# Attention sums guarded on VectorE across partitions, all probability copies on ScalarE

## The chip, the cores and the metric

The kernel runs on one core of one Trainium2 chip. The metric is the device time of that core in microseconds (us), the median of the runs shown. One execution was profiled; its trace is what is read here.

## The reference

There are 8 batches, 8 heads, a sequence of 576 and a head size of 64. Causal attention with a decay is followed by a layer in which 128 of the 576 tokens of each batch go through a two-layer network.

```python
scores = scale * np.matmul(q, k.transpose(0, 1, 3, 2))
cum = np.cumsum(np.log(np.clip(f, 0.0001, 1.0)), axis=-1)
scores = np.where(causal, -1e9, scores + cum[..., :, None] - cum[..., None, :])
attn = np.exp(scores - scores.max(-1, keepdims=True))
attn = attn / (attn.sum(-1, keepdims=True) + 1e-09)
x = heads_side_by_side(attn @ v)                  # per batch 576 x 512
s = x @ w_gate
top = the 128 tokens of the batch with the largest s
out = x;  out[top] += sigmoid(s[top]) * (relu(x[top] @ w1) @ w2)
```

## The kernel before

**Pairs of heads.** The 64 heads are worked in 32 pairs `p`, two heads on the two halves of the partitions. For each pair `pair_ops` loads q and k through SyncE's queue (L533 to L540) and, for each head, the row of decays broadcast over 128 partitions (L554); GpSimd makes the masked forms of that row (L453, four instructions a head, called the masks below). `pair_parts` then has TensorE compute scores in groups of rows (L642); VectorE adds decay or mask, keeps the row maximum and writes to SBUF (L686, called the passes); ScalarE takes the exponential in place and adds up its row sums (L734) into a small tile `st`; TensorE transposes the exponentials into PSUM (L753); they are copied into `pt` in SBUF (the probability copies, helper `copy_on`, L380 on ScalarE and L384 on VectorE); TensorE multiplies them with v (L834); ScalarE moves the result to SBUF (`both`, L380).

**The odd blocks.** 576 is four blocks of 128 and one of 64. The 64 rows of block `NF` of the two heads share one exponential: the sums of the first head come to partitions 0 to 63 and those of the second to partitions 64 to 127 of the same column of `st`. The probability copies of block `i == 0` contain those 64 rows as well: they are four copy instructions (`cps`, for `hh` 0 and 1), which before go to ScalarE for even pairs and to VectorE for odd pairs (`other`). The copies of blocks 1, 2 and 3 (`cp`, two instructions each) go to ScalarE.

**The sums.** In `back_parts` the sums of the second head's 64 rows are first moved to the partitions 0 to 63 by a transfer on SyncE's queue (`side_b`, L872). Then GpSimd adds 1e-9 and writes the result to `rn` (`guard`, L875), and VectorE takes the reciprocal (`inv`, L878). `rn` is used when the attention output, transposed back (L904), is normalised (`norm`, L909). After that GpSimd multiplies by w_gate (`gate`, L918), and VectorE adds up (`gsum`, L923; for a whole batch `router`, L926).

**The network.** For each batch the gate values are transposed and broadcast (L1006, or L1034 for the last batch), VectorE ranks the tokens (L1051) and makes a selection matrix (L1059), TensorE turns it into indices (L1083), GpSimd gathers the rows by an indirect DMA (L1095), TensorE transposes and multiplies (L1117, L1166, L1173, L1196, L1225, L1233), and GpSimd scatters the rows back (L1244). This cannot begin before all weights are loaded and split into a high and a low part on GpSimd (L980, L983).

**The order.** Nothing of the order is written out as a loop. Every step is handed to `Flow.add` with a cost per engine, what it comes after, what buffers it takes and gives, and a `place`; `Flow.run` simulates the engines and always issues, of the steps that could start within `EPS` us of the earliest, the one with the lowest place (plus `GW` times a price for changing the kind of matmul on TensorE). A step with two engines goes where its estimated end plus a bias is earlier; the bias on VectorE is `BD`. The constants from `BD` to `GL` (L214 to L280) set these places. On each engine the instructions then run in exactly the order issued: an instruction that waits holds everything behind it on its engine. The loads of SyncE's queue are in this order too.

Of the kernel before, what the change touches and what calls it, by code (L numbers as in the profile page):

```python
# [15 lines left out]
ALU = mybir.AluOpType  # L16
PSUM = bass.MemoryType.PSUM

P = 128
# [12 lines left out]
class Flow:  # L32
# [32 lines left out]
    def add(self, cost, fn, after=(), place=0.0, take=(), give=(), lat=0.0, kind=None, dma=None):  # L65
        t = {"dma": dma, "cost": cost, "fn": fn, "place": place, "take": take, "give": give, "lat": lat, "kind": kind,
             "wait": 0, "next": [], "deps": [], "end": None, "eng": None, "n": self.todo}
        for d in after:
            if d is None:
                continue  # L70
            t["deps"].append(d)
            d["next"].append(t)
            t["wait"] += 1
        self.todo += 1
        if t["wait"] == 0:
            self.ready.append(t)
        return t
# [101 lines left out]
def kernel(  # L179
# [16 lines left out]
    nc = tc.nc  # L196
# [7 lines left out]
    NF = S // P  # L204
    R = S - NF * P
# [5 lines left out]
    NRT = (cap + P - 1) // P  # L211
    FR = 3 * R

    BD = 20.076  # L214
    WP = 17
    WQ = 0
    R0 = -95.926
    X0 = -56.195
    XE_ = -552.713
    XH_ = 149.767  # L220
    XM_ = -169.727
    XB_ = -6.848
    XN_ = -241.558
    XO_ = -378.371
    XU_ = 1.133
    XQ_ = 841.132
    XR_ = 432.401
    XG_ = 282.534
    PL4 = -232.452
    GW = 72.274  # L230
    EPS = 0.195
    LOOK = 13
    PR = -446.374
    PL = -33.455
    PS = 1944.004
    PV = 248.52
    PW_ = -45.48
    PM = -161.276
    PE_ = 157.486
    PC = -335.036  # L240
    PB = -145.984
    PD = -36.798
    VO = -5.988
    VD = 1
    GD = 0.1
    WS = -165.794
    WD = 748.358
    LL = 123.925
    A0 = 1.528
    A1 = 28.648  # L250
    A2 = 13.447
    A3 = 15.65
    A4 = 28.136
    A5 = -20.066
    A6 = -18.73
    A7 = 70.066
    M0 = -10.589
    M1 = -23.402
    M2 = 3.697
    M3 = -16.245  # L260
    M4 = 13.276
    M5 = 6.769
    M6 = 116.943
    M7 = -86.187
    N0 = -21.109
    N1 = -29.883
    N2 = -33.246
    N3 = -4.275
    N4 = -85.647
    N5 = 88.993  # L270
    N6 = 234.387
    N7 = -85.431
    WL = 320.113
    RK = 82.406
    RD = -4.884
    XP = 29.412
    GO = 40.352
    GS = 2.404
    GL = -142.634
    LG = 2.69  # L280
    SB = 3
    SX = 2.5
# [41 lines left out]
    sts = [const.tile([P, NCH, 2], F32, name=f"st{r}") for r in range(3)]  # L324
# [44 lines left out]
    def act(n):  # L369
        return {"act": n / 1200 + 0.05}  # L370

    def dve(n):
        return {"dve": n / 960 + 0.065}
# [16 lines left out]
    add = flow.add  # L390

    def load(fn, kb, n=1, slow=0.0, **kw):
        return add({"sp": 0.63 * n}, fn, lat=1.6 + slow, dma=kb / 240, **kw)
# [45 lines left out]
    def t_warm(e):  # L439
# [9 lines left out]
                give=[tk_ep])  # L449
# [5 lines left out]
    def t_late(e):  # L455
# [14 lines left out]
                 after=[d_ident], place=-59)  # L470
# [23 lines left out]
    d_rows = add({"pool": 1.8}, t_rows, place=-49.4)  # L494
    d_clear = add({"pool": 0.4}, t_clear, after=[d_ep], place=-18)
# [94 lines left out]
    d_wg, invs, avd, avb, tails = [], [], {}, {}, {}  # L590
    normed, gjd = {}, []

    def pair_parts(p):
# [19 lines left out]
        copied = []  # L613
        sums = []
        exps, late, scored, ready, tk_nm = {}, {}, {}, {}, {}
        plan = []
        for u, group in enumerate(groups):
            t = p * NT + (AT[u] - LOOK) // 2
# [3 lines left out]
            place = p * NU + AT[u] * XU_ - LOOK * NU / 8  # L622
# [31 lines left out]
        for u, i, k0, k1, co, x2, tk_b, place in plan:  # L654
# [36 lines left out]
            for hh in range(2):  # L691
# [17 lines left out]
                for g, (a, b_, in1, what) in enumerate(todo):  # L709
# [6 lines left out]
                    elif first:  # L716
# [3 lines left out]
                             after=[x3] + src + ([ready[hh, i]] if (hh, i) in ready and not first else [])  # L720
                             + ([ready[0, i]] if i == NF and hh else []),
                             place=place + PM + XH_ * hh + 0.01 * g, take=[tk_nm[hh, i]] if first and not (i == NF and hh) else [], give=[tk_b[hh]] if lastp else [])
# [13 lines left out]
                w = R + (i + 1) * P if i < NF else R  # L736
# [7 lines left out]
        for i in (3, 1, 2, 0):  # L744
            t = p * NU + (4, 1, 2, 0)[i] + XB_
            tk_t = Token("ps", 2, 2)
            w = (i + 1) * R

            def tr(e, i=i, w=w, tk_t=tk_t):
                tp = st["tp", i] = pair(tk_t)  # L750

                def turn(g, col, src):
                    nc.tensor.transpose(tp[:, g, col:col + R], src, ident[g * R:g * R + R, g * R:g * R + R])  # L753

                for hh in range(2):
                    t_ = st["pw", i if i > 1 else i + 2]
                    for j in range(i + 1):
                        o = PAT[i] + j * P + hh * (WB[i] + R)
                        for g in range(2):
                            turn(g, hh * w + R * j, t_[g * R:g * R + R, o:o + P])  # L760
                if i == 0:
                    for g in range(2):
                        turn(g, 2 * R, p4s[p % 2][g * R:g * R + R, (1 - g) * R:(1 - g) * R + P])
                    for c in range(NF):
                        o = PAT[c] + (c + 1) * P
                        turn(1, (3 + c) * R, st["pw", c if c > 1 else c + 2][R:P, o:o + P])

            def cp(e, i=i, hh=0, w=w):
                dst = pts[p]
                tp = st["tp", i]  # L770
                src = tp[:, :, hh * w:hh * w + w].rearrange("p g (j c) -> p j g c", c=R)
                o, step = (R + P * i, 512) if hh == 0 else (2624 + R - 512 * i, 640)
                d_ = dst[:, o:o + 1]
                copy_on(e, bass.AP(dst.tensor, d_.offset, [d_.ap[0], [step, i + 1], [R, 2], [1, R]]), src)

            def cps(e, hh):
                dst = pts[p]
                tp = st["tp", 0]
                o, step = (640, 640) if hh == 0 else (2112, -512)
                d_ = dst[hh * R:hh * R + R, o:o + 1]  # L780
                copy_on(e, bass.AP(dst.tensor, d_.offset, [d_.ap[0], [step, NF], [1, R]]),
                        tp[hh * R:hh * R + R, 1, 3 * R:(3 + NF) * R].rearrange("p (j c) -> p j c", c=R))
                if hh == 0:
                    d_ = dst[:, R:R + 1]
                    copy_on(e, bass.AP(dst.tensor, d_.offset, [d_.ap[0], [2624, 2], [R, 2], [1, R]]),
                            tp[:, :, 0:2 * R].rearrange("p g (h c) -> p h g c", c=R))
                else:
                    d_ = dst[:, 0:1]
                    copy_on(e, bass.AP(dst.tensor, d_.offset, [d_.ap[0], [2624, 2], [1, R]]), tp[:, :, 2 * R:3 * R])

            if i == 0:
                ex_all = [exps[hh, c] for hh in range(2) for c in range(NF)] + [exps[1, NF]]
                x5 = add(turns(7), tr, after=ex_all + [d_pt, d_ident], place=t, take=[tk_t],
                         give=[late[2], late[3], late[NF]], kind="turn")
            else:
                x5 = add(turns(2 * i + 2), tr, after=[exps[0, i], exps[1, i], d_pt, d_ident], place=t, take=[tk_t],
                         give=[late[i if i > 1 else i + 2]], kind="turn")
            for hh in range(2):
                other = i == 0 and p % 2 == 1
                if i == 0:  # L800
                    n_ = 4 * P - 2 * R * hh
                    x6 = add({"dve": n_ / 960 + 0.13} if other else {"act": n_ / 1200 + 0.22}, lambda e, cps=cps, hh=hh: cps(e, hh), after=[x5, d_rows] + (copied if other else []),
                             place=t + PC + 0.01 * hh, give=[tk_t])
                else:
                    x6 = add(dve(2 * w) if other else act(2 * w), lambda e, cp=cp, hh=hh: cp(e, hh=hh), after=[x5, d_rows] + (copied if other else []),
                             place=t + PC + 0.01 * hh, give=[tk_t])
                copied.append(x6)
            moved.append(x5)


# [54 lines left out]
    def back_parts(p, st, wdone, at, sums, d_l, tk_ot, joint):  # L865
# [2 lines left out]
        wdone = wdone + [joint]  # L868
        rn = rns[b % 2][:, :, 2 * hp:2 * hp + 2]

        def side_b(e):
            nc.sync.dma_start(out=sts[p % 3][0:R, NF, 1:2], in_=sts[p % 3][R:P, NF, 0:1])  # L872

        def guard(e):
            nc.gpsimd.tensor_scalar(rn, sts[p % 3], 1.0, 1e-9, ALU.mult, ALU.add)  # L875

        def inv(e):
            nc.vector.reciprocal(rn, rn)  # L878


        bp = at - VO + (PD if odd else PB)
        gt = gates[b]
        d_lb = load(side_b, 24, slow=SB, after=[d_l], place=9 * p + 4 - LOOK + PL4)
        d_inv = add({"pool": 0.25}, guard, after=sums + [d_lb, d_clear] + invs[-1:], place=bp - 2 - XM_ + XG_,
                    take=[gt["tk"]] if hp == 0 and NRT else [])
        invs.append(d_inv)
        d_inv = add({"dve": 0.14}, inv, after=[d_inv], place=bp - 2)


        hb, w_ = divmod(hp, NP // 2)  # L890
# [431 lines left out]
```

## Time and profile before

| what | value |
|---|---|
| median of 3 runs | 415.38 us (414.71 to 418.03) |
| the profiled execution's own time | 415.3 us |
| its span | 413.6 us |
| TensorE busy | 388.1 us, 94% |
| ScalarE busy | 311.8 us, 75% |
| VectorE busy | 299.4 us, 72% |
| GpSimd busy | 217.2 us, 53% |

The profile names engines PE (TensorE matmuls), PEld (TensorE weight loads), DVE (VectorE), ACT (ScalarE), POOL (GpSimd) and SP (SyncE). Busy time is the union of the instructions of an engine in a stretch, so a stretch's length less the busy time is that engine's idle time. PEclk is the granted clock of TensorE as a share of its full 2.4 GHz; 0.50 is the lower level, 1.2 GHz. "A <- B" in the view of waits means that A's engine sat idle before A until B ended.

### The profile page before, as it was taken

Reading aid. Unit: us, or ns where it says so; the run is one execution under the profiler, and the core shown is the slowest. Engines: PE = TensorE matmul, PEld = TensorE weight load, DVE = VectorE, ACT = ScalarE, POOL = GpSimd, SP = SyncE. Lnnn points to the kernel's source line nnn. Section 1 sums busy time; section 2 is a strip of 40 time slices with the busy share of each in tenths; the row PEclk is TensorE's granted clock in tenths of the full one; section 3 lists DMA queues with packets and bytes.
Section 4 is the critical chain, followed back from the end, with each engine's and each line's share of the span. In section 5 each row is a group of like instructions: output and inputs, shape, how many; then the busy total and the mean of one; then the engine's idle time right before and its main releaser. Section 6 shows DMA issues by size and latency. Waiting matters only on the chain.

```text
span 413.6 us, 11932 instructions
## 1 busy us (share of the span) xinstructions
PE 388.1 (94%) x3979; PEld 267.0 (65%) x3979; DVE 299.4 (72%) x1109; ACT 311.8 (75%) x945; POOL 217.2 (53%) x387
## 2 busy tenths in 40 slices
PE   6799999999995999999999999999999999999994
PEld 4566656556663676767666675757575766767773
DVE  3666868697984588987949894898699669638402
ACT  4889999999994799857977889968798779323220
POOL 3787886696929482637436372646463622131101
PEclk9879999999996999999999999999999999999998
DMA  5997988698896484746648574567884521111101
GB/s 162 230 254 220 252 229 216 186 270 214 229 242 188 124 255 110 229 129 169 189 116 225 151 206 136 171 191 194 216 231 136 133 61 52 59 54 56 52 0 51
DMA packets 76867, 68.08 MB, mean 165 GB/s; under 512 B 47715, under 2 KB 56966, under 8 KB 76806
## 3 DMA queue, kind: packets, MB, share of 16 engines
q1 hardware_dynamic: 75446, 62.98, 55.8%
q0 software_dynamic: 1280, 4.20, 3.3%
q8 instruction: 31, 0.51, 0.5%
q14 instruction: 30, 0.25, 0.2%
q10 hardware_dynamic: 80, 0.15, 0.1%
HBM read 55.59 MB, written 11.70 MB: 163 GB/s over the span
## 4 chain that ended last, share of the span: by engine, by line
PE 62%; issue 10%; DVE 9%; ACT 6%; DMA 5%; POOL 5%; SPq 1%; POOLq 0%; ACTq 0%; DVEq 0%
PE banks L834 18%; PE banks L642 17%; PE banks L753 9%; PE banks L1166 5%; PE banks L1225 4%; DVE p L686 4%; POOL m L453 3%; ACT pt L380 3%; PE banks L1173 2%; PE banks L1233 2%; ACT p L734 2%; DMA xe<-out_dram,idx 2%; PE banks L904 1%; DVE x L909 1%; DMA out_dram<-xe,idx 1%
## 5 line engine op out<-in xcount | busy, mean ns | idle before, releaser
L734 ACT ACTIVATE p<-p,nm 128x320 f32<-128x320 f32 (+4 forms) x288 | 166.4, 587 | 22.6 <-DVE nm L686 22.2
L453 POOL TENSOR_SCALAR_AFFINE_SELECT m<-e 128x320 f32<-128x320 f32 (+3 forms) x256 | 108.9, 454 | 88.8 <-DVE nm L686 52.0
L642 PE MATMUL banks<-rk,rq 64*128 64x192 f32 (+4 forms) x768 | 119.9, 424 | 4.7 <-ACT e L380 1.6
L686 DVE CUSTOM_DVE_ANT_0 p<-banks,m 128x320 f32<-128x320 f32 (+3 forms) x256 | 100.8, 418 | 21.9 <-PE banks L642 13.8
L380 ACT COPY pt<-banks 128x256 f32<-128x256 f32 (+4 forms) x256 | 99.1, 453 | 16.0 <-PE banks L753 14.5
L834 PE MATMUL banks<-pt,v 128*64 128x448 f32 (+4 forms) x768 | 92.7, 392 | 0.0
L642 PEld LDWEIGHTS banks<-rk,rq 64*128 64x128 f32 x768 | 70.9, 193 | 22.8 <-DVE nm L686 4.2
L753 PEld LDWEIGHTS banks<-ident,p 64*128 64x128 f32 x1472 | 60.9, 141 | 28.3 <-ACT pt L380 8.4
L753 PE MATMUL banks<-ident,p 64*128 64x64 f32 x1472 | 71.8, 231 | 6.6 <-ACT pt L380 2.1
L834 PEld LDWEIGHTS banks<-pt,v 128*64 128x64 f32 x768 | 47.0, 137 | 44.3 <-issue 29.9
L918 POOL TENSOR_TENSOR gj<-x,wg 128x640 f32<-128x640 f32 x32 | 50.1, 1579 | 29.2 <-DVE x L909 28.3
L734 ACT ACTIVATION_READ_ACCUMULATOR p<-p,nm 128x1 f32 x288 | 56.8, 197 | 0.0
L686 DVE CUSTOM_DVE_ANT_0 p<-banks,e 128x384 f32<-128x384 f32 x64 | 34.5, 552 | 16.7 <-PE banks L642 8.2
L1051 DVE SCALAR_TENSOR_TENSOR j<-srow,sg,later 128x576 uint8<-128x576 f32 (+1 forms) x40 | 34.0, 851 | 1.0
L686 DVE CUSTOM_DVE_ANT_0 p<-banks,m,nm 128x192 f32<-128x192 f32 x64 | 26.4, 413 | 10.4 <-PE banks L642 6.4
L380 ACT COPY both<-banks 128x448 f32<-128x448 f32 (+1 forms) x47 | 22.2, 487 | 15.3 <-PE banks L834 15.1
L909 DVE TENSOR_TENSOR x<-banks,rn 128x640 f32<-128x640 f32 x32 | 25.6, 820 | 8.1 <-ACT p L734 4.3
L686 DVE DVE_READ_ACCUMULATOR2_ANT nm<- 128x1 f32 (+1 forms) x384 | 31.1, 81 | 0.0
L923 DVE TENSOR_REDUCE gu<-gj 128x5 f32<-128x640 f32 x32 | 25.8, 813 | 3.6 <-POOL gj L918 3.5
L1225 PE MATMUL banks<-w2h,hth 128*128 128x512 f32 x64 | 26.9, 420 | 0.0
L1166 PE MATMUL banks<-w1h,xth 128*128 128x512 f32 x64 | 26.7, 418 | 0.0
L1244 POOL DMA_INDIRECT out_dram<-xe,idx x8 | 8.2, 1029 | 33.8 <-DVE xe L1240 32.8
(85 smaller groups left out, 390.0 us busy)
## 6 DMA issues: line engine op xcount, KB each, us to landing
e<-eq SPq DMA_DIRECT2D x62, 288.0 KB
rk<-in_qk_dram SPq DMA_DIRECT2D x32, 288.0 KB
out_dram<-x SPq DMA_DIRECT2D x16, 512.0 KB
rq<-in_qk_dram SPq DMA_DIRECT2D x32, 144.0 KB
rq<-in_qk_dram SPq DMA_DIRECT2D x32, 128.0 KB
v<-in_v_dram SPq DMA_DIRECT2D x32, 128.0 KB
v<-in_v_dram SPq DMA_DIRECT2D x32, 80.0 KB
srow<-sd SPq DMA_DIRECT2D x7, 320.0 KB
```

The lines of the kernel that those rows point to most:

```text
L380: nc.scalar.copy(d, s_)
L453: nc.gpsimd.affine_select(out=dst, in_=src, pattern=w, compare_op=ALU.is_ge, fill=NEG, base=base, channel_multiplier=1)
L642: nc.tensor.matmul(st["sc", u][hh][:, o:o + k1 - k0], q_rows(raws["q", p], hh, i), raws["k", p][rows, k0:k1], start=True, stop=True)
L686: nc.vector.tensor_tensor_reduce(out=into(hh, i, r_, x0, x1), in0=blocks(b_[r_, x0 - k0:x1 - k0], hh, i), in1=blocks(in1(), hh, i), scale= ...
L734: nc.scalar.activation(x, x, AF.Exp, bias=st["nm", hh, i], scale=-1.0, accum_out=l)
L753: nc.tensor.transpose(tp[:, g, col:col + R], src, ident[g * R:g * R + R, g * R:g * R + R])
L834: nc.tensor.matmul(avb[p, g][par * D:(par + 1) * D, qo + q0 - g * SPL:qo + q1 - g * SPL], vt[:, j, par * D:(par + 1) * D], pt[:, off:off + ...
L909: nc.vector.tensor_tensor(out=xhs[key][:, :, w_ * P:(w_ + 1) * P].rearrange("p c (h d) -> p c h d", h=2), in0=st["tb"][:, :, 0:NCH * D].re ...
L918: (nc.vector if e == "dve" else nc.gpsimd).tensor_tensor(out=gjs[p % 2], in0=xhs[key][:, :, w0:w1], in1=wg[:, hb * HB + w0:hb * HB + w1].u ...
L1051: nc.vector.scalar_tensor_tensor(junk[0:n, :], st["srow"][0:n, 0:S], sg()[0:n, c:c + 1], later[0:n, o:o + S], ALU.subtract, ALU.is_gt, acc ...
L1166: nc.tensor.matmul(q["hp", n][0:nr, :], q["xth"][:, c, 0:nr], r_[:, c, cs], start=(c == 0 and k_ == 0), stop=False)
L1225: nc.tensor.matmul(q["yp"][0:nr, :], q["hth"][:, c, 0:nr], r_[:, c, :], start=(c == 0 and k_ == 0), stop=False)
```

## The change

The transfer and GpSimd's instruction are gone; VectorE makes the guard itself, in two instructions, the second of which reads partitions 64 to 127 and writes partitions 0 to 63. The step now has a cost on VectorE alone and a place of its own. The probability copies of block 0 may go to either engine by cost, for all pairs alike, and those of blocks 1 to 3 too in the pairs before the twelfth; two halves are one step now. With the bias of 17.9 us on VectorE, as the change names it, all of them are on ScalarE. Of some 60 constants of places nearly all are new.

```diff
-    BD = 20.076
+    BD = 17.906
...
-    XE_ = -552.713
+    XE_ = -744.767
...
-    PL4 = -232.452
-    GW = 72.274
-    EPS = 0.195
+    PL4 = 145.164
+    GW = 50.716
+    EPS = 0.036
...
-            for hh in range(2):
-                other = i == 0 and p % 2 == 1
-                if i == 0:
-                    n_ = 4 * P - 2 * R * hh
-                    x6 = add({"dve": n_ / 960 + 0.13} if other else {"act": n_ / 1200 + 0.22}, lambda e, cps=cps, hh=hh: cps(e, hh), after=[x5, d_rows] + (copied if other else []),
-                             place=t + PC + 0.01 * hh, give=[tk_t])
-                else:
-                    x6 = add(dve(2 * w) if other else act(2 * w), lambda e, cp=cp, hh=hh: cp(e, hh=hh), after=[x5, d_rows] + (copied if other else []),
-                             place=t + PC + 0.01 * hh, give=[tk_t])
-                copied.append(x6)
+            if i == 0:
+                def both_halves(e, cps=cps):
+                    cps(e, 0)
+                    cps(e, 1)
+
+                n_ = 8 * P - 2 * R
+                copied = [add({"dve": n_ / 960 + 0.26, "act": n_ / 1200 + 0.44}, both_halves, after=[x5, d_rows] + copied,
+                              place=t + PC, give=[tk_t, tk_t])]
+            elif p < 12:
+                def both_heads(e, cp=cp):
+                    cp(e, hh=0)
+                    cp(e, hh=1)
+
+                copied = [add({"dve": 4 * w / 960 + 0.13, "act": 4 * w / 1200 + 0.1}, both_heads, after=[x5, d_rows] + copied,
+                              place=t + PC, give=[tk_t, tk_t])]
+            else:
+                for hh in range(2):
+                    copied.append(add(act(2 * w), lambda e, cp=cp, hh=hh: cp(e, hh=hh), after=[x5, d_rows],
+                                      place=t + PC + 0.01 * hh, give=[tk_t]))
...
-        def side_b(e):
-            nc.sync.dma_start(out=sts[p % 3][0:R, NF, 1:2], in_=sts[p % 3][R:P, NF, 0:1])
-
-        def guard(e):
-            nc.gpsimd.tensor_scalar(rn, sts[p % 3], 1.0, 1e-9, ALU.mult, ALU.add)
-
         def inv(e):
+            nc.vector.tensor_scalar(rn, sts[p % 3], 1.0, 1e-9, ALU.mult, ALU.add)
+            nc.vector.tensor_scalar(rn[0:R, NF, 1:2], sts[p % 3][R:P, NF, 0:1], 1.0, 1e-9, ALU.mult, ALU.add)
             nc.vector.reciprocal(rn, rn)
...
-        d_lb = load(side_b, 24, slow=SB, after=[d_l], place=9 * p + 4 - LOOK + PL4)
-        d_inv = add({"pool": 0.25}, guard, after=sums + [d_lb, d_clear] + invs[-1:], place=bp - 2 - XM_ + XG_,
+        d_inv = add({"dve": 0.36}, inv, after=sums + [d_clear] + invs[-1:], place=bp + PL4,
                     take=[gt["tk"]] if hp == 0 and NRT else [])
         invs.append(d_inv)
-        d_inv = add({"dve": 0.14}, inv, after=[d_inv], place=bp - 2)
```

## Rows read from the trace of the kernel before

**Rows 1.** The page, busy time of each engine over the span.
```profile
PE 388.1 (94%) x3979; PEld 267.0 (65%) x3979; DVE 299.4 (72%) x1109; ACT 311.8 (75%) x945; POOL 217.2 (53%) x387
```

**Rows 2.** Windows by stage: length, PE, PEld, DVE, ACT, POOL busy, clock, DMA, GB/s.
```profile
0.00:30.00 30.00, 23.21 (x174) 16.48 (x176) 16.68 (x75) 20.79 (x59) 20.19 (x57) 0.89 0.82 217
30.00:120.00 90.00, 84.08 (x1041) 56.02 (x1038) 72.16 (x292) 87.36 (x277) 68.85 (x112) 1.00 0.87 227
...
131.00:343.00 212.00, 209.72 (x2222) 141.96 (x2222) 169.53 (x636) 174.53 (x534) 107.92 (x197) 0.99 0.59 167
...
361.00:414.00 53.00, 47.21 (x324) 34.97 (x322) 20.16 (x43) 11.24 (x23) 9.12 (x8) 0.97 0.12 42
```

**Rows 3.** Waits between 119 and 131 us: total, times, longest.
```profile
PE banks L1006 <- DVE sg L926: 5.0, 1, 5.0
DVE rn L878 <- POOL rn L875: 4.8, 1, 4.8
...
POOL m L453 <- DMA xe<-out_dram,idx: 4.4, 1, 4.4
```

**Rows 4.** Timeline of VectorE around that wait: start, length, instruction, [idle before].
```profile
121.62 1.49 DVE L384 COPY pt<-banks 64x256 f32<-64x256 f32 x4
127.88 0.22 DVE L878 RECIPROCAL rn<-rn 128x10 f32<-128x10 f32 x1 [4.76 <-POOL rn L875]
...
129.56 0.17 DVE L926 TENSOR_REDUCE sg<-gu 128x5 f32<-128x20 f32 x1
```

**Rows 5.** Timeline of GpSimd over the same stretch.
```profile
108.44 4.03 POOL L453 TENSOR_SCALAR_AFFINE_SELECT m<-e 128x384 f32<-128x384 f32 x8
...
118.22 1.44 POOL L453 TENSOR_SCALAR_AFFINE_SELECT m<-e 128x384 f32<-128x384 f32 x3
124.10 0.24 POOL L453 TENSOR_SCALAR_AFFINE_SELECT m<-e 64x64 f32<-64x64 f32 x1 [4.44 <-DMA xe<-out_dram,idx]
...
125.92 1.63 POOL L453 TENSOR_SCALAR_AFFINE_SELECT m<-e 128x384 f32<-128x384 f32 x4
127.64 0.21 POOL L875 TENSOR_SCALAR rn<-st 128x10 f32<-128x10 f32 x1
```

**Rows 6.** Windows of 2 us across the wait, columns as in rows 2.
```profile
124.00:126.00 2.00, 0.76 (x14) 0.34 (x10) 0.00 (x0) 0.00 (x0) 1.82 (x3) 1.00 1.01 325
...
130.00:132.00 2.00, 2.00 (x21) 1.61 (x22) 1.91 (x3) 1.57 (x5) 1.92 (x4) 0.50 0.59 146
132.00:134.00 2.00, 2.00 (x10) 1.29 (x10) 0.57 (x2) 1.15 (x5) 1.85 (x6) 0.50 0.18 40
134.00:136.00 2.00, 2.00 (x28) 1.19 (x26) 1.57 (x7) 1.18 (x3) 2.00 (x4) 0.86 0.43 148
```

**Rows 7.** Groups by shape on ScalarE, 30 to 120 us: busy, mean ns, idle.
```profile
L380 ACT COPY pt<-banks 128x256 f32<-128x256 f32 x27 | 9.2, 390 | 0.8 <-PE banks L753 0.8
...
L380 ACT COPY pt<-banks 64x256 f32<-64x256 f32 x10 | 3.7, 372 | 0.4 <-PE banks L753 0.2
...
L380 ACT COPY pt<-banks 128x128 f32<-128x128 f32 x5 | 1.3, 266 | 0.1
```

**Rows 8.** Windows of line L384 alone: length, DVE busy (instructions), clock, DMA, GB/s.
```profile
30.00:120.00 90.00, 7.33 (x20) 1.00 0.87 227
131.00:343.00 212.00, 13.10 (x36) 0.99 0.59 167
```

**Rows 9.** Groups by shape on VectorE, the whole span.
```profile
L878 DVE RECIPROCAL rn<-rn 128x10 f32<-128x10 f32 x32 | 6.7, 209 | 11.4 <-POOL rn L875 11.4
...
L1138 DVE TENSOR_SCALAR g<-g 128x1 f32<-128x1 f32 x8 | 1.1, 143 | 0.0
...
L469 DVE TENSOR_SCALAR pick<-ident 64x2 f32<-64x2 f32 x1 | 0.1, 96 | 0.0
```

**Rows 10.** Waits of VectorE, 130 to 400 us: total, times, longest.
```profile
DVE rn L878 <- POOL rn L875: 6.6, 4, 3.0
```

**Rows 11.** Waits of SyncE's queue, the whole span.
```profile
SPq L872 <- ACT p L734: 25.2, 17, 11.6
```

More of the change, by code (lines that the diff above doesn't have):

```diff
@@ L212 @@
     FR = 3 * R
-    BD = 20.076
+    BD = 17.906
     WP = 17
     WQ = 0
-    R0 = -95.926
-    X0 = -56.195
-    XE_ = -552.713
[L220 to L228, printed above, removed]
-    PL4 = -232.452
-    GW = 72.274
-    EPS = 0.195
-    LOOK = 13
[L233 to L243, printed above, removed]
+    R0 = -43.969
+    X0 = -89.689
+    XE_ = -744.767
+    XH_ = 120.288
+    XM_ = -28.125
+    XB_ = -7.023
+    XN_ = -525.252
+    XO_ = -533.822
+    XU_ = 1.155
+    XQ_ = 922.165
+    XR_ = 244.889
+    XG_ = 498.561
+    PL4 = 145.164
+    GW = 50.716
+    EPS = 0.036
+    LOOK = 13
+    PR = -1009.237
+    PL = -168.62
+    PS = 1939.642
+    PV = 415.631
+    PW_ = -278.549
+    PM = -109.584
+    PE_ = 280.036
+    PC = -243.721
+    PB = -70.016
+    PD = -37.925
+    VO = -4.182
     VD = 1
     GD = 0.1
[L246 to L279, printed above, removed]
+    WS = -258.495
+    WD = 601.345
+    LL = 213.987
+    A0 = 4.556
+    A1 = 15.448
+    A2 = 12.281
+    A3 = 10.371
+    A4 = 39.555
+    A5 = 17.375
+    A6 = -212.803
+    A7 = -123.525
+    M0 = -24.955
+    M1 = 7.883
+    M2 = -2.963
+    M3 = -34.632
+    M4 = 48.216
+    M5 = -250.257
+    M6 = 255.509
+    M7 = -79.069
+    N0 = 49.864
+    N1 = -58.185
+    N2 = -44.668
+    N3 = -2.382
+    N4 = -105.954
+    N5 = 36.782
+    N6 = 16.302
+    N7 = -38.636
+    WL = 343.323
+    RK = 84.175
+    RD = -1.805
+    XP = 12.611
+    GO = 40.913
+    GS = 1.925
+    GL = -201.092
     LG = 2.69
```

## The prediction

> **What bounds the kernel now.** I read the page's busy line first. TensorE is busy 388.1 of 413.6 us [rows 1], so 25.5 us of idle time, and whatever TensorE loses at the lower clock, is nearly all that a change of this kind can win: the matmuls themselves stay. The page does not say where those 25.5 us are, so the windows by stage come next [rows 2]. There the reader is to see four stages. In the first 30 us 6.8 us are idle (loads and set-up). From 30 to 120 us TensorE idles 5.9 us and ScalarE only 2.6 us (90 less 87.36): with no network work to do yet, ScalarE is the tighter of the two. From 131 to 343 us TensorE idles 2.3 us in 212 while ScalarE has 37 us free: TensorE bound. The tail from 361 idles about 5.4 us (47.21 of the 52.6 us up to the end of the span), the last scatter among it. What is left lies between 120 and 131 us, and there the view of waits shows one single stop of TensorE of 5.0 us [rows 3]. I then followed this stop back through the timelines, and I read the clock behind it in windows of 2 us.
>
> **The stop at 125 us.** TensorE waits for VectorE's `sg` (L926). VectorE was not busy: after its copies, which end at 123.11, it stood at the reciprocal of the sums for 4.76 us, and only then could it do the passes behind it and reach `sg` at 129.56 [rows 4]. The reciprocal waited for GpSimd's guard, at 127.64. GpSimd had stood 4.44 us before a small mask, until 124.10, and then made a gate product and more masks before it came to the guard [rows 5]. So a 0.21 us instruction at the end of a held queue stopped VectorE, which stopped TensorE. After the stop TensorE runs at 0.50, the 1.2 GHz level, from 130 to 134 and at 0.86 to 136 [rows 6]: half of 4 us and 0.14 of 2 us, or 2.0 + 0.3 = 2.3 us, are lost on top. The whole stop costs 7.3 us.
>
> **The change part by part.**
>
> Guard on VectorE. VectorE no longer waits for GpSimd in the reciprocal. From 123.11 on it makes the guard (about 0.3 us, below) and does what it did from 127.88 on: 129.56 less 127.88 is 1.7 us up to `sg`. So `sg` starts at 123.1 + 0.3 + 1.7 = 125.1 instead of 129.56, and TensorE's idle time falls from 5.0 to 0.5 us (129.56 less 125.1 is 4.5). From 30 to 120 us many short stops add up to 5.9 us and leave the clock at 1.00 [rows 2], so I count the 2.3 us as won: 4.5 + 2.3 = 6.8 us. What is late next are the masks of the second head of the following pair, which GpSimd ends at 127.55 [rows 5]; the first head's were made from 118.22 to 119.66, and in this kernel TensorE's scores for that pair need only their space, so VectorE meets the late masks a few passes after `sg`, about when they are there. The bounds are 0 (the masks hold VectorE just as long) and 7.3. I take 6.8.
>
> The other waits for the guard, 6.6 us in four cases [rows 10], fall into the stage where TensorE idles 2.3 us in 212: VectorE's passes are early enough there to cover them. I take 0; the end below is -2.3.
>
> The guard's cost. The trace has no instruction that moves values across partitions on VectorE. The nearest rows are a TENSOR_SCALAR of 128x1 at 143 ns, one of 64x2 at 96 ns and the reciprocal of 128x10 at 209 ns [rows 9]. Two instructions therefore cost 0.19 to 0.42 us a pair; I take 0.29 by the first row, 32 x 0.29 = 9.3 us in all. It is covered, for VectorE gives up the copies of the odd pairs, 1.49 us each [rows 4], 16 x 1.49 = 23.8 us. VectorE is thus relieved by about 14 us. TensorE gets nothing of this by itself: VectorE has 18 us free from 30 to 120 us already [rows 2]. If that cover were gone, the guard would take up to 32 x 0.42 = 13.4 us of VectorE, still inside the 18 + 42 us that it has free from 30 to 120 and from 131 to 343 us.
>
> The copies on ScalarE. An odd pair adds two copies of 64x256, one of 128x256 and one of 128x128: 2 x 0.372 + 0.390 + 0.266 = 1.40 us [rows 7]. From 30 to 120 us five odd pairs had these copies on VectorE, 20 instructions [rows 8], so ScalarE gets 5 x 1.40 = 7.0 us more in a stage where it had 2.6 us free. The rest, 7.0 - 2.6 = 4.4 us, makes the stage longer, and TensorE idles for it, since the network's first matmuls come only after this stage. The ends are 0 (the new order hides the copies, or gives TensorE network work sooner) and 7.0 (the free time cannot be used, because it is itself waiting for transposes), with 1.4 on top for the sixth odd pair, at 121.62, where ScalarE was idle anyway. I take 4.4. From 131 to 343 us nine odd pairs, 36 instructions [rows 8], add 12.6 us to ScalarE's 174.5 of 212: 88%, beneath TensorE's 99%. I take 0; the upper end is 2, as much again as TensorE idles there.
>
> A page has another price for these copies: the Trainium skill, "ScalarE: Activation LUTs", section "Rules for kernel authors", budgets about 0.3 us for each ACTIVATE and 0.83 ns for each element, an estimate of 4 x 0.3 + 896 x 0.00083 = 1.94 us for the four. By it the stage would grow by 9.7 - 2.6 = 7.1 us and the sum would come to 415.6. The rows have the same copies, from PSUM on ScalarE, at 1.40 us, so the trace does not agree and I stay with it.
>
> The transfer. SyncE's queue loses 32 issues and the places where it stood behind one, 25.2 us in 17 cases [rows 11]; loads behind them can start sooner. From 131 us on TensorE hardly waits for anything [rows 2], and before that ScalarE, which needs no load, is the tighter engine. I take 0; the end below is -1.
>
> The places. Every step may change its neighbours, and this has no row. What it can win is bounded by TensorE's remaining idle time between 30 and 343 us, 5.9 + 2.3 = 8.2 us; what it can lose I set at another stop like the one above, 7.3 us. I take 0.
>
> **The sum.** -6.8 + 4.4 = -2.4 us. The profiled execution took 415.3 us, so the forecast is 412.9; the median of the runs, 415.38, stands 0.1 above that execution, which changes nothing. One per cent is 4.15 us, about what a measurement of this kernel can tell from no change: 411.2 and 419.5 are the borders.
>
> **Rivals.**
>
> *The copies are hidden* (faster). The stop goes, and ScalarE's 7.0 us are taken up by the new order, or the copies of some pairs stay on VectorE after all, which the costs would allow. 415.3 - 6.8 = 408.5; with a few of the 8.2 us of small stops won too, 405. For it: TensorE and ScalarE are nearly balanced in that stage, 84.1 against 87.4, and VectorE's in-order stops get fewer. Against: 2.6 us of room for 7.0 us of work.
>
> *ScalarE's room cannot be used.* Nothing hides, and the five pairs cost their full 7.0: 415.3 - 6.8 + 7.0 = 415.5. For it: the room is short waits in front of copies. The page named above gives nearly the same time by its price.
>
> *The stop stays and ScalarE is longer* (slower). GpSimd was held until 124.10 by something that lands in memory, not by the guard, and the masks behind it are still its work. If VectorE meets the first of these before it reaches `sg`, it stands until 126 or later all the same, TensorE's clock falls as before, and nothing is won, while the copies cost 4.4 to 8.4 us: 419.7 to 423.7, about 421. It decides from the point where the passes queued before `sg` need a mask made after 124.10. For it: masks are made only just ahead of use here. Against: the passes that follow the reciprocal belong to the pair whose masks, eight of them, were made from 108.44 to 112.47 [rows 5].
>
> **How the numbers follow.** I give the forecast 0.36, the hidden copies 0.32, the unusable room 0.12, the stop that stays 0.20. The forecast's own range is 410 to 416, and a tenth of it lies under 411.2. Faster by over 1%: 0.32 + 0.04 = 0.36. Slower by over 1%: 0.20. Within 1%: 0.44. The range reaches from 405.5 to 421.0, over most of the hidden copies and half of the slower case, and leaves out about 2 in 10.
>
> **What would show it.** Right: no idle time of VectorE in front of the guard, no stop of TensorE over 2 us between 30 and 343 us, its clock at 1.00 throughout; ScalarE at 98% or more up to 120 us and the first matmuls of the network at about the same time with some 4 us less of attention done by then; from 131 us TensorE at 99%. Wrong: a new stop of several microseconds with the clock at 0.50 behind it; ScalarE with free time before 120 us while TensorE still idles; probability copies in VectorE's line; VectorE's guard instructions far over 0.2 us each; or TensorE's busy sum moving by more than 2 us, which would mean that the order of matmul kinds, not the stops, set the difference.

## The result and the profile after

The changed kernel takes 411.16 us (410.43 to 414.30, 19 runs) beside 415.38 us before (412.33 to 418.03, 19 runs): a ratio of 0.9897, 95% interval 0.9879 to 0.9914. That is 4.3 us or 1.03% less, on the border that the prediction drew at 1% (the interval is 0.86% to 1.21%). The forecast was 412.9 us and the range, 405.5 to 421.0, holds the result. A median counts all runs, a ratio only those in the faster of two states of the chip. As the experiments show, the sum came out near for reasons that were only partly those given.

The busy line of the changed kernel's page answers to [rows 1]:

```profile
PE 390.5 (95%) x3979; PEld 263.3 (64%) x3979; DVE 287.7 (70%) x1109; ACT 327.0 (80%) x1009; POOL 214.8 (52%) x355
```

The span is 410.6 us instead of 413.6. TensorE is busy 2.4 us longer and idles 20.1 us instead of 25.5. The same windows by stage as in [rows 2], with the stretch of the stop added:

```profile
0.00:30.00 30.00, 23.52 (x160) 17.91 (x160) 15.83 (x73) 19.79 (x55) 19.52 (x55) 0.83 0.83 216
30.00:120.00 90.00, 84.01 (x985) 54.79 (x983) 67.58 (x283) 86.89 (x282) 67.87 (x103) 1.00 0.84 231
120.00:131.00 11.00, 11.00 (x120) 7.45 (x120) 9.07 (x38) 10.89 (x35) 9.41 (x13) 1.00 0.76 205
131.00:343.00 212.00, 210.46 (x2234) 138.32 (x2231) 164.42 (x646) 187.27 (x586) 104.32 (x174) 1.00 0.59 166
...
361.00:414.00 53.00, 43.51 (x285) 32.89 (x281) 19.32 (x43) 10.42 (x21) 8.05 (x7) 0.97 0.12 42
```

Between 120 and 131 us TensorE is busy all the time and its clock is 1.00: the stop of [rows 3] and the half clock of [rows 6] are gone. From 30 to 120 us TensorE idles 6.0 us, as before, although ScalarE has the copies of the odd pairs too. From 131 us on ScalarE is at 187.3 of 212 us, 88%, as worked out, and TensorE idles 1.5 us instead of 2.3. The first 30 us have a clock of 0.83 instead of 0.89. The difference is a stretch from 10 to 14 us, where the kernel before has 1.00:

```profile
10.00:12.00 2.00, 2.00 (x10) 1.79 (x12) 0.84 (x3) 0.55 (x2) 1.93 (x5) 0.64 0.77 183
12.00:14.00 2.00, 2.00 (x8) 1.50 (x7) 1.04 (x6) 0.58 (x1) 1.79 (x8) 0.51 0.57 159
```

Counted in windows of 2 us, as busy time times the missing share of the clock, the lower levels cost TensorE 4.35 us in the first 30 us (1.7 of it here) instead of 3.1, and after that nothing instead of 2.4. So at the full clock its 3979 matmuls would be busy about 386.2 us in the changed kernel and 382.6 before, an estimate from these windows: it has less idle time, but its matmuls take 3.5 us longer.

The view of TensorE's waits over the whole span has nothing long in it any more; its first lines are:

```profile
PE banks L753 <- ACT pt L380: 3.7, 6, 1.0
PE banks L433 <- DVE both L407: 1.9, 1, 1.9
PE banks L1086 <- DVE oh L1062: 1.2, 1, 1.2
```

The groups by shape show the new instructions on VectorE, which answer to [rows 9]:

```profile
L883 DVE RECIPROCAL rn<-rn 128x10 f32<-128x10 f32 x32 | 6.9, 217 | 1.1
L881 DVE TENSOR_SCALAR rn<-st 128x10 f32<-128x10 f32 x32 | 5.1, 160 | 10.6 <-ACT p L734 10.5
...
L882 DVE TENSOR_SCALAR rn<-st 64x1 f32<-64x1 f32 x32 | 4.8, 149 | 1.1
```

The two guards take 0.16 + 0.15 = 0.31 us a pair; 0.29 was taken. One more thing moved. The transposes of the network's first gathered rows (L1117 before, L1120 after) start 15 us earlier. The first line is the kernel before (its second profiled execution, below):

```profile
124.15 0.46 PE L1117 MATMUL banks<-ident,xe 64*128 64x64 f32 x8
```

and this one is the changed kernel:

```profile
109.01 0.46 PE L1120 MATMUL banks<-ident,xe 64*128 64x64 f32 x8
```

### The profile page after: what moved, and what is told of

Same layout as the page of the kernel before. It is cut to its first block, busy times and chain, and to the rows that moved or that the text cites. A ratio compares the mean times of both kernels' runs of the same rounds, so it can differ in the third digit from the quotient of the medians.

```text
span 410.6 us, 11848 instructions
## 1 busy us (share of the span) xinstructions
PE 390.5 (95%) x3979; PEld 263.3 (64%) x3979; DVE 287.7 (70%) x1109; ACT 327.0 (80%) x1009; POOL 214.8 (52%) x355
## 4 chain that ended last, share of the span: by engine, by line
PE 59%; ACT 17%; issue 10%; DVE 8%; DMA 2%; SPq 1%; POOL 1%; POOLq 0%; ACTq 0%; DVEq 0%
PE banks L642 17%; PE banks L843 14%; ACT p L734 10%; PE banks L753 9%; ACT pt L380 6%; PE banks L1228 5%; PE banks L1169 5%; DVE p L686 3%; PE banks L1176 2%; PE banks L1236 2%; DVE j L1054 2%; PE banks L907 2%; DMA rq<-in_qk_dram 2%; DVE x L912 1%; ACT both L380 1%
## 5 line engine op out<-in xcount | busy, mean ns | idle before, releaser
L453 POOL TENSOR_SCALAR_AFFINE_SELECT m<-e 128x384 f32<-128x384 f32 (+3 forms) x256 | 115.0, 478 | 76.8 <-DVE nm L686 40.9
L380 ACT COPY pt<-banks 64x256 f32<-64x256 f32 (+3 forms) x320 | 120.8, 430 | 17.4 <-PE banks L753 15.9
L686 DVE CUSTOM_DVE_ANT_0 p<-banks,m 64x64 f32<-64x64 f32 (+3 forms) x256 | 101.1, 418 | 24.6 <-PE banks L642 15.8
L642 PEld LDWEIGHTS banks<-rk,rq 64*128 64x128 f32 x768 | 69.5, 192 | 19.2 <-DVE nm L686 4.7
L843 PEld LDWEIGHTS banks<-pt,v 128*64 128x64 f32 x768 | 45.5, 137 | 47.9 <-issue 31.2
L1169 PE MATMUL banks<-w1l,xth 128*128 128x512 f32 x64 | 25.2, 393 | 0.0
```

Of the source, the lines that this page charges most:

```text
L380: nc.scalar.copy(d, s_)
L453: nc.gpsimd.affine_select(out=dst, in_=src, pattern=w, compare_op=ALU.is_ge, fill=NEG, base=base, channel_multiplier=1)
L642: nc.tensor.matmul(st["sc", u][hh][:, o:o + k1 - k0], q_rows(raws["q", p], hh, i), raws["k", p][rows, k0:k1], start=True, stop=True)
L686: nc.vector.tensor_tensor_reduce(out=into(hh, i, r_, x0, x1), in0=blocks(b_[r_, x0 - k0:x1 - k0], hh, i), in1=blocks(in1(), hh, i), scale= ...
L843: nc.tensor.matmul(avb[p, g][par * D:(par + 1) * D, qo + q0 - g * SPL:qo + q1 - g * SPL], vt[:, j, par * D:(par + 1) * D], pt[:, off:off + ...
L1169: nc.tensor.matmul(q["hp", n][0:nr, :], q["xth"][:, c, 0:nr], r_[:, c, cs], start=(c == 0 and k_ == 0), stop=False)
```

## The experiments

The change does three things at once: it moves the guard, it moves the copies, and it lays everything out in a new order. To tell them apart, most of these kernels keep the planner's steps, costs and places, so that the order of all other instructions stays, and change only what a step issues. Every ratio is to the kernel before, measured on the same chip. Where ratios are turned into microseconds below, they are taken of 415.38 us.

**Is the stop at 125 us a property of the order?** The kernel before, unchanged, was profiled again.

> The kernel before, unchanged, profiled a second time. If the stop of TensorE near 125 us belongs to the order (theory), it is there again with 4 to 6 us and the half clock behind it. If it was an accident of that one execution (rival), it is under 2 us here, and taking it away could never have won 6.8 us of the median.

It took 412.69 us in its one run. The view of waits has the stop again, 4.3 us long:

```profile
PE banks L1006 <- DVE sg L926: 4.3, 1, 4.3
```

Its windows of 10 us show what the clock did, and how full VectorE (third busy column) is ahead of the stop:

```profile
100.00:110.00 10.00, 9.28 (x94) 5.42 (x96) 9.56 (x37) 9.23 (x30) 9.60 (x14) 1.00 0.98 255
110.00:120.00 10.00, 9.28 (x137) 7.02 (x133) 9.83 (x37) 9.79 (x33) 5.61 (x10) 1.00 0.82 201
120.00:130.00 10.00, 5.66 (x68) 3.74 (x67) 5.71 (x24) 6.02 (x19) 6.42 (x10) 0.92 0.92 262
130.00:140.00 10.00, 10.00 (x94) 6.53 (x92) 5.01 (x19) 8.79 (x28) 6.15 (x13) 0.91 0.48 128
```

So the stop belongs to the order. The clock behind it costs less this time: 0.09 of the 10 us from 130 us on, 0.9 us, instead of the 2.3 us of [rows 6].

**The guard alone.** The first try had VectorE do all three instructions where the reciprocal stood.

```diff
-            nc.sync.dma_start(out=sts[p % 3][0:R, NF, 1:2], in_=sts[p % 3][R:P, NF, 0:1])
...
-            nc.gpsimd.tensor_scalar(rn, sts[p % 3], 1.0, 1e-9, ALU.mult, ALU.add)
...
+            nc.vector.tensor_scalar(rn, sts[p % 3], 1.0, 1e-9, ALU.mult, ALU.add)
+            nc.vector.tensor_scalar(rn[0:R, NF, 1:2], sts[p % 3][R:P, NF, 0:1], 1.0, 1e-9, ALU.mult, ALU.add)
             nc.vector.reciprocal(rn, rn)
```

> Before's order kept to the instruction; only the transfer and GpSimd's guard are left out and VectorE does its two guard instructions where the reciprocal stood. Theory (the guard on GpSimd made the stop at 125 us): the stop of 5.0 us and its half clock go, 415.4 - 6.8 = 408.6 us, no wait of VectorE before the guard over 1 us. Rival (masks on GpSimd hold VectorE just as long, or the load was late anyway): 414 to 416 us, with a stop of 4 to 5 us still near 125 us. Rival (it is the new order alone that helped): 414 to 416 us too, but with the stop gone and its time lost elsewhere.

It gave 1.0037 (1.0010 to 1.0064). But in this order later exponentials may be issued ahead of that point, so some reciprocals can be made from the sums of a later pair: part of the computation is changed, and the run can't decide. It was repeated with the two guards at the guard's own step, where the sums are still the right ones, and the reciprocal left at its place.

> Before's order; VectorE makes the guard at the moment at which the order issues GpSimd's guard, so that the next use of the sums still comes after it, and the reciprocal stays where it is. Transfer and GpSimd's guard are gone. Theory as far as it still stands (the stop at 125 us was the guard's): no stop of TensorE over 2 us at 120 to 131 us, clock 1.00 there, 408.6 to 411 us. Rival (what the stop gives back is lost again, because the order was laid out for a guard on GpSimd and VectorE now waits for sums in front of its passes): 414 to 417 us, with several waits of VectorE for ScalarE's sums of 1 us and more.

0.9985 (0.9954 to 1.0015), 415.05 us: no gain that can be told from nothing. In its windows of 10 us the stop is smaller, but time is lost in front of it, and the clock falls there:

```profile
100.00:110.00 10.00, 7.68 (x90) 4.64 (x89) 9.66 (x33) 8.23 (x29) 9.78 (x14) 1.00 0.81 241
110.00:120.00 10.00, 9.95 (x122) 5.72 (x119) 8.80 (x38) 8.04 (x25) 0.99 (x3) 0.83 0.53 158
120.00:130.00 10.00, 8.66 (x113) 5.71 (x110) 9.51 (x35) 9.69 (x31) 6.96 (x11) 1.00 0.72 236
```

The waits between 98 and 112 us say what TensorE stands for there, and VectorE's timeline why it is late:

```profile
PE banks L753 <- DVE pt L384: 2.1, 1, 2.1
```

```profile
102.83 0.15 DVE L875 TENSOR_SCALAR rn<-st 128x10 f32<-128x10 f32 x1
103.01 0.15 DVE L876 TENSOR_SCALAR rn<-st 64x1 f32<-64x1 f32 x1
...
105.27 1.90 DVE L1052 SCALAR_TENSOR_TENSOR j<-srow,sg,later 64x576 uint8<-64x576 f32 x1
...
108.09 1.49 DVE L384 COPY pt<-banks 64x256 f32<-64x256 f32 x4
```

VectorE's timeline marks no idle time from 98 to 110 us. It carries the guards and the ranking of the first batch in one queue with the odd pair's copies; these start at 108.09 (106.36 in the first profile of before), and TensorE waits for them to empty its banks (its output space in PSUM). Not all of the 1.7 us is the guards': the ranking instruction of 1.90 us took 1.07 in the first profile of before. Neither the theory (408.6 to 411) nor the wait for sums that the rival named is what happened: VectorE's idle time in front of its guards is nil here.

**Is it VectorE's time?** The same order with no guard on any engine. The transfer and the reciprocal at its old place are gone too (not shown below), so the rows of the second head's 64 sums are left out of the normalisation; the tile of the sums starts at 1.

```diff
-            nc.vector.memset(t, 0.0)
+            nc.vector.memset(t, 1.0)
...
-            nc.gpsimd.tensor_scalar(rn, sts[p % 3], 1.0, 1e-9, ALU.mult, ALU.add)
+            nc.vector.reciprocal(rn, sts[p % 3])
```

> Before's order; no transfer and no guard on any engine, the reciprocal alone is made from the sums at the guard's step (the 1e-9 and the second head's first 64 sums are left out, so those rows are not normalised). VectorE has two instructions of 0.15 us a pair less than in the run with the guard at its step. If the guard's time on a VectorE that is 97% busy between 100 and 120 us is what ate the gain: 409 to 412 us. If the gain is gone whatever VectorE has to do (the time was lost to the order): 413.5 to 415.5 us, no different from the run with the guard at its step.

0.9851 (0.9801 to 0.9902), 410.64 us, so VectorE's guards it was. Against the run above, VectorE's busy time is 299.3 instead of 309.7 us, and the kernel is 0.9985 - 0.9851 = 1.34% faster, 5.6 us: about half of VectorE's added 10.4 us reaches the end. The two profiled executions differ by less, 414.06 - 411.82 = 2.2 us. The odd pair's copies start at 107.08 here, so 1.0 us of their delay above belongs to the guards (the ranking has one instruction of 1.70 us here too). The lines of `sg`, the first without guards and the second with them, show how far VectorE's queue is behind by the time of the stop:

```profile
125.36 0.17 DVE L926 TENSOR_REDUCE sg<-gu 128x5 f32<-128x20 f32 x1
```

```profile
128.25 0.17 DVE L927 TENSOR_REDUCE sg<-gu 128x5 f32<-128x20 f32 x1
```

The wait for GpSimd is worth 1 - 0.9851 = 1.49%, 6.2 us. The profile shows less, 415.3 - 411.8 = 3.5 us, in part because the clock falls from 130 to 140 us here too (0.83).

**Does the transfer cost anything?** The transfer was kept and only GpSimd's step removed, with VectorE's one reciprocal made straight from the sums at that step; the tile of the sums starts at 1 here too.

> Before's order with the transfer on SyncE's queue kept; only GpSimd's guard goes, and VectorE's one reciprocal is made straight from the sums at the guard's step (1e-9 added to a sum of at least 1 changes nothing in 32-bit numbers), so VectorE has no instruction more than before. If the wait for GpSimd is the whole price and the transfer costs nothing (theory): as the run without any guard, ratio 0.982 to 0.990, 408 to 412 us. If the transfer's place in SyncE's queue or its landing costs as well (rival): 413 to 416 us.

0.9861 (0.9790 to 0.9932), 411.93 us. The transfer costs nothing that can be measured. Its profile against that of before, 408.9 against 415.3 us, has TensorE idle 4.1 us less and busy 2.3 us less, with a clock of 1.00 from 120 to 140 us. This kernel computes all that the reference wants, keeps every place of before, and is as fast as the changed kernel; the two intervals overlap, so it can't be called faster. Its windows by stage show that the gain over [rows 2] is in the middle stretch and behind it:

```profile
30.00:120.00 90.00, 83.86 (x1036) 55.80 (x1034) 72.14 (x291) 87.10 (x277) 66.47 (x104) 1.00 0.85 232
120.00:131.00 11.00, 9.56 (x115) 6.55 (x112) 9.24 (x36) 9.81 (x31) 8.05 (x12) 1.00 0.81 219
131.00:343.00 212.00, 210.63 (x2260) 143.81 (x2257) 172.41 (x650) 177.21 (x543) 101.38 (x177) 1.00 0.61 167
```

**The copies alone.** The odd pairs' copies of block 0 on ScalarE, all else as before.

```diff
-                    x6 = add(... lambda e, cps=cps, hh=hh: cps(e, hh), ...
+                    x6 = add(... lambda e, cps=cps, hh=hh: cps("act", hh), ...
```

> Before's order kept; only the odd pairs' copies of block 0 go to ScalarE, guard and transfer as before. Theory (ScalarE is the tight engine up to 120 us, 7.0 us more on it against 2.6 us free): 415.4 + 4.4 = 419.8 us, ScalarE over 98% busy from 30 to 120 us. Rival (hidden): 414 to 416.5 us. Rival (no free time usable): 422 us.

1.0153 (1.0107 to 1.0198), 422.24 us: 6.4 us slower, between the theory's 4.4 and the full 7.0. Its windows from 30 to 120 us and from 131 to 343 us, and TensorE's longest waits:

```profile
30.00:120.00 90.00, 80.04 (x975) 51.54 (x970) 62.34 (x257) 88.55 (x282) 64.51 (x107) 1.00 0.83 224
...
131.00:343.00 212.00, 206.85 (x2183) 140.40 (x2183) 157.34 (x595) 183.13 (x568) 107.91 (x198) 0.99 0.60 167
```

```profile
PE banks L642 <- ACT pt L380: 5.2, 7, 1.4
PE banks L753 <- ACT pt L380: 4.6, 7, 1.1
```

ScalarE is at 88.6 of 90 us, and TensorE idles 10.0 us instead of 5.9 because its banks are emptied late. It also idles 5.2 instead of 2.3 us from 131 us on, where ScalarE has 29 us free and nothing was charged. The stop is still there, at 2.4 us.

**Both edits in the old order.** First with all three instructions at the reciprocal's place, with the same reservation as above:

> Before's order with both edits in place. Theory (they add up, places worth nothing): 415.4 - 6.8 + 4.4 = 413.0 us. If the measured 411.2 us of the change needs the new order, this lies 1 to 3 us above it; if the copies are hidden, 408 to 410 us.

1.0134 (1.0089 to 1.0179). Then with the guards at their own step:

> The same with the odd pairs' copies of block 0 on ScalarE, in before's order. Theory (the edits add up, with the 6.3 us that the copies cost in place): the run with the guard alone + 6.3 us. If the copies' cost shrinks once the guard is gone, less than that.

1.0102 (1.0057 to 1.0146), 419.49 us. On top of the guard alone the copies cost 1.0102 - 0.9985 = 1.17%, 4.9 us, which can't be told from the 6.4 us that they cost alone (each term is some 2 us wide to either side). TensorE's waits for the copies are as in the run with the copies alone, 5.1 and 3.9 us. So the change's edits, without its places, make the kernel 4.2 us slower.

**The places.** Two kernels were planned anew, each with the other's constants: first the changed kernel's steps with the constants of before, then the steps of before with the changed kernel's constants.

> The changed kernel's steps, planned with before's constants (the sums' step at the reciprocal's old place). Theory of the places (a set of places is worth something only with the steps it was found for): 418 to 426 us, well above both kernels. Rival (the edits carry the gain, places worth nothing): 410 to 414 us.

> Before's steps (transfer, GpSimd's guard, odd copies on VectorE), planned with the changed kernel's constants (the transfer's place kept). Theory of the places: 418 to 426 us. Rival (the new places are simply better): 410 to 414 us.

1.0544 (1.0499 to 1.0589), 437.89 us, and 1.0352 (1.0297 to 1.0406), 429.38 us, both slower even than the theory's 418 to 426. Here a set of places is worth something only with the steps that it was found for. Between the edits in the old order and the changed kernel lie 1.0102 - 0.9897 = 2.05%, 8.5 us, and that is the new order (with the merged copy steps that belong to it).

**The copies in the new order.** In the changed kernel the odd pairs' copies went back to VectorE, all else in its place.

```diff
                 def both_halves(e, cps=cps):
+                    e = "dve" if p % 2 else e
```

> The changed kernel's order kept; only the odd pairs' copies of block 0 go back to VectorE in place. Theory (ScalarE is still tight up to 120 us and its 7.0 us are paid there): 411.2 - 4.4 = 406.8 us. Rival (the new order hides the copies, the network starting at 109 us instead of 124 us fills TensorE): 410 to 412.5 us.

1.0184 (1.0144 to 1.0224), 423.65 us, 11.9 us slower than the changed kernel by the difference of the ratios and far outside both expectations. Like the edits in the old order, it is made in an order that was laid out without it. Its windows and TensorE's longest wait:

```profile
30.00:120.00 90.00, 81.48 (x947) 53.36 (x945) 70.62 (x291) 78.99 (x251) 67.24 (x102) 0.98 0.83 227
...
131.00:343.00 212.00, 203.23 (x2156) 135.12 (x2154) 168.94 (x652) 169.91 (x522) 102.03 (x171) 1.00 0.58 162
```

```profile
PE banks L642 <- DVE nm L686: 6.3, 8, 1.4
```

ScalarE has 11 us free from 30 to 120 us and TensorE still idles 8.5. What is late now are VectorE's passes, which stand behind the copies in their queue: here TensorE idles 8.8 us from 131 us on, with VectorE at 80%.

**VectorE's time in the new order.** The two guards and the reciprocal became two reciprocals straight from the sums.

```diff
-            nc.vector.tensor_scalar(rn, sts[p % 3], 1.0, 1e-9, ALU.mult, ALU.add)
-            nc.vector.tensor_scalar(rn[0:R, NF, 1:2], sts[p % 3][R:P, NF, 0:1], 1.0, 1e-9, ALU.mult, ALU.add)
-            nc.vector.reciprocal(rn, rn)
+            nc.vector.reciprocal(rn, sts[p % 3])
+            nc.vector.reciprocal(rn[0:R, NF, 1:2], sts[p % 3][R:P, NF, 0:1])
```

> The changed kernel's order; instead of two guards and a reciprocal, two reciprocals straight from the sums (1e-9 added to a sum of at least 1 changes nothing in 32-bit numbers), one VectorE instruction of 0.16 us a pair less. If VectorE's queue still sets part of the time before 120 us: 409.5 to 410.8 us. If TensorE and ScalarE alone set it: 411.0 to 411.5 us.

0.9903 (0.9863 to 0.9942), 412.12 us, the same as the changed kernel. In the new order an instruction less on VectorE is worth nothing that can be measured; there VectorE has given up the odd pairs' copies, and TensorE's longest wait for it is 1.2 us.

## Why the prediction came out

| term | forecast | measured | from |
|---|---|---|---|
| wait for GpSimd and the transfer gone | -6.8 | -6.2 | no guard at all |
| guards on VectorE | 0 | +5.6 | guard at its step, less no guard |
| copies on ScalarE | +4.4 | +4.9 | both, less guard at its step |
| places | 0 | -8.5 | changed kernel, less both |
| sum | -2.4 | -4.2 | |

The measured terms add up to the measured ratio by construction (4.3 us, but for rounding). Each single term is some 2 us wide to either side, since the intervals of the runs are up to 0.5% to either side, and the terms hang on the order in which the edits are taken: by the copies alone (+6.4) and then the guard (1.0102 - 1.0153, -2.1), the split is another. That the sum came within 2 us of the result is luck: two terms taken at 0 were 5.6 and -8.5 us and nearly cancel.

**The stop.** The chain from the small mask through the guard, the reciprocal and `sg` to TensorE was right, and the size too: 6.2 us against 6.8. `sg` starts at 125.36 in the run without any guard, where 125.1 was worked out, and at 128.25 in the one with VectorE's guards. The part of it that is the clock's varies from execution to execution: the cost of the lower levels from 120 to 140 us is 2.4 and 1.35 us in the two profiles of before, 1.7 with no guard and nothing with the transfer kept (same count in windows of 2 us). The rival in which the stop stays falls: in each of the runs without the wait for GpSimd TensorE idles at most 1.8 us between 120 and 131 us. What lands in memory still holds GpSimd there, but VectorE no longer stands behind it.

**The guards' cost.** This is the step that failed: taking the guards at 0, because even with no cover they were "still inside the 18 + 42 us that it has free". With the copies still on VectorE they cost 5.6 us. The reserve, VectorE's 18 us free in 90, was an average over the stage. Between 100 and 120 us VectorE is 97% busy in the kernel before (9.56 + 9.83 of 20 us), just ahead of the stop, and there 0.3 us a pair push the copies and passes behind them. The sum should have had an end of the whole 32 x 0.29 = 9.3 us for this term. Whether giving up the copies covers the guards, as the prediction says first, is not shown in the old order: there the copies alone shrink the stop to 2.4 us, moving the guard as well wins 2.1 us with an interval that reaches past 0, and no run has the copies on ScalarE and no guard. In the new order the cover holds as far as one instruction of three can show it: 0.9903 without it against 0.9897.

**The copies.** The size fits, 4.9 us against 4.4, and 6.4 with the guard still on GpSimd, but the account behind it only in part. Up to 120 us it holds: the copies alone add 4.0 us to TensorE's idle time there. From 131 us on they add 2.9 us more, where 0 was taken with an upper end of 2. The rival of the unusable room, 7.0, lies inside the interval of the copies alone (4.4 to 8.2) and is not ruled out. The price from the Trainium skill ("ScalarE: Activation LUTs", "Rules for kernel authors"), 7.1 us for this term as an estimate by its budget for an ACTIVATE, does not agree with the traces: by it a copy of 128x256 would take an estimated 0.51 us, and the changed kernel's have a mean of 0.38 us (0.39 in [rows 7]). That budget is stated for an ACTIVATE with its bias as a pointer operand, and these are COPY instructions, so it need not hold for them. The 6.4 us of the copies alone come near to its sum by another way, TensorE's waits from 131 us on.

**The places.** Nothing was charged, with 8.2 us as the most that the idle time would allow. The new order won 8.5 us over the old one with the same edits, which had opened more idle time first: TensorE idles 28.3 us in the run with both edits in the old order (416.8 less 388.5) and 20.1 us in the changed kernel. TensorE is busy 2.0 us longer in exchange, so the two profiles differ by 6.2 us. The prediction's end for the copies, network work sooner, came true: the network's rows are transposed at 109 us, and from 120 to 131 us TensorE is full. But it is not shown to be the whole cause: of the idle time won back 3.0 us lie between 30 and 100 us, ahead of that, 3.1 between 100 and 140 and 3.9 from 140 to 344 us (the set-up and the tail lose 1.7). Which of the constants does it, no run separates.

**Signs set beforehand.** No stop over 2 us from 30 to 343 us and a clock of 1.00 there: so it is. ScalarE at 98% or more up to 120 us and the network at the same time: no, 96.5% and 15 us earlier. No idle time of VectorE before the guard: no, 10.5 us in ten waits for ScalarE's sums, but with no wait of TensorE for VectorE over 1.2 us behind them after the set-up. TensorE's busy sum moved by 2.4 us, more than the 2 that was to mean that the order of the matmul kinds counts; with the clock taken out it is 3.5 us. So this sign of being wrong came true. But by the same count the run with both edits in the old order has 385.6 us already, so most of it is not the new order's; what it is made of is open.

## What to carry to other kernels

An engine's free time in a long stage is no cover: read it in the windows just ahead of the wait that is to go, in the order in which the queue runs there. Taking a wait out and putting work on the engine that waited are two edits with two prices, and here they cancelled; the cheaper way to the same time was to drop the instruction that had caused the wait, since adding 1e-9 to a sum of at least 1 does nothing in 32-bit numbers. And where an order is laid out by hand or by a planner, an edit costs what it does to that order: judge it after the order is found anew, and don't read the total as the price of the edit.

## What the runs showed of the hardware

VectorE reads partitions 64 to 127 and writes partitions 0 to 63 in one TENSOR_SCALAR of 64x1 in 149 ns, no more than the 160 ns of the 128x10 that stays in its partitions.

A ranking instruction of 64x576 took 1.90 us at 105.27 in the run with the guard at its step, where the median of all forty is 0.82. GpSimd's timeline has a product of two inputs over the first 1.27 us of it:

```profile
105.29 1.27 POOL L984 TENSOR_TENSOR w2l<-wst,w2h 128x512 fp32r<-128x512 f32 x1
```

The Trainium skill, "GPSIMD Engine Reference", section "1. Specifications", says that GpSimd shares its way into SBUF with VectorE and that VectorE's instructions with two SBUF inputs contend with it; the ranking has two such inputs. This one instance agrees; no run here separates it from other causes.

The clock of the first 30 us was 0.89 in the two profiles of before and 0.83 in all three that keep the new order. In the changed kernel it fell to 0.64 and 0.51 between 10 and 14 us, after TensorE had been busy 1.06 of the 2 us from 8 to 10; the kernel before was busy only 0.50 there and kept 1.00 until 18 us. Two other kernels had 0.83 too, the first try of the guard alone in the old order and the new steps with the old places, so it is not the new order alone; the cause is open.
